# Four low halves of the output weights: subtracted on VectorE in round 0, where GpSimd subtracted them in the first routing

## The chip, the cores and the metric

The kernel runs on one core of a Trainium2 chip, as one program. The metric is device time in microseconds (us), from launch to end; the profile's span runs from the first to the last instruction and is a little shorter. The engines are TensorE (PE; PEld is its weight load), VectorE (DVE), ScalarE (ACT), GpSimd (POOL) and SyncE (SP, which issues plain DMAs). Each engine works through its own queue in order.

## The reference, cut to what matters

Three stages follow each other. The tokens are 3072 rows of 320 numbers.

```python
# 1. recurrent attention, 4 x 8 heads, 768 steps, head size 40  -> x[3072, 320]
# 2. routing: each token to one of 8 experts, at most 384 tokens each
logits = x @ w_gate
order = np.argsort(-logits.flatten())
for idx in order:
    tok, e = idx // 8, idx % 8
    if assigned[tok] >= 0 or counts[e] >= 384: continue
    assigned[tok] = e; counts[e] += 1
for e in range(8):
    out[assigned == e] = np.maximum(x[assigned == e] @ w1[e], 0) @ w2[e]   # 320 -> 1024 -> 320
# 3. a dense layer for all tokens
h = out @ w_in                                          # 320 -> 2048
g = np.where(h > 0, h, np.exp(np.minimum(h, 0)) - 1)
y = g @ w_out                                           # 2048 -> 320
```

`w_in` and `w_out` arrive as 64-bit floats.

## The kernel before, in words

**Stages.** First the attention runs (24 units, to about 160 us). Then the first routing finds the expert that is filled first and its 384 tokens. Then come eight rounds, one for each expert in the order in which they are filled. A round gathers its 384 rows of x and its expert's weights, does the expert's two matmul layers (P1 up, C1 down), and goes on at once with the dense layer for the same rows (P2 up, C2 down) and scatters the result. Routing r+1 is computed on VectorE beside round r.

**High and low halves.** For accuracy every matmul operand is split into a high part, which TensorE's reduced format holds exactly, and the low rest: h = round(F), l = F - h, with three products hh, lh and hl summed. So every weight and activation costs a copy (h) and a subtraction (l).

**The output weights.** `w_out` is cut into 16 pieces of 128x320. Since the chip gets 64-bit words, a piece is first rebuilt as 32-bit floats: ACT takes the exponent and the sign from the upper word (L867, L869), DVE shifts the lower word (L872) and joins the parts with an exclusive-or (L879), and GpSimd multiplies by the sign (L882), or DVE works the sign in with one more instruction (L876). Then ACT or DVE copies the high half (L980 or L982) and GpSimd subtracts the low half (L973). Pieces 0 to 6 (EARLY = 7) are done during the attention. Pieces 7 to 15 are done by the generator `wout_pieces`: as many as fit in the first routing, the rest in round 0. Round 0 needs piece f first in its C2 step f.

**The first routing.** It is a loop of counting steps: DVE compares all tokens with 32 thresholds (ge, L563, 128x768 bf16), TensorE counts, DVE folds the counts over the partitions (L587 to L593) and picks the next digit (L746, L749). `start` issues these steps, and wherever a step marks a gap for TensorE (k > FK) it advances `wout_pieces` up to its next stop for DVE; a yield's second value names the engines that the next part wants:

```python
while True:
    d = "d" in need
    _, need = next(fill)
    if d and "d" in need:
        break
```

When the routing has its expert, GpSimd gathers that expert's w1 (L991), then the rows of x.

**Order in the rounds.** A planner (`Plan`) keeps a clock and a booked time per engine (a, d, p), from fixed costs of each instruction, and the order of issue follows it. After `start` it is reset. `main` issues matmuls, two or a few per step; after each step `run` first issues the dependent work that is due (such as gl of P1, L1127) and then offers a turn to four side generators in the order `wout routes rows weights`. A generator's turn goes on as long as its next yield is not in the future and the engine that it names is not booked more than its slack ahead of the clock (wout 2000, weights 1000, routes and rows 3000 and 600). Between C1's last step and C2's first (`rush`) only routing may go on. `main` holds C2 of round 0 back until `wdone` says that the piece is issued. `weights` splits the gathered expert weights (L980, L987), `rows` gathers, transposes and splits the tokens of the next round (xh, xl, L1064).

Of the kernel before, what the change touches and what calls it, by code (L numbers as in the profile page):

```python
# [8 lines left out]
F32 = mybir.dt.float32  # L9
# [4 lines left out]
ALU = mybir.AluOpType  # L14
# [13 lines left out]
EARLY = 7  # L28
# [790 lines left out]
class Mlp:  # L819
# [128 lines left out]
    def wout_pieces(self):  # L948

        nc = self.nc  # L950
        wide = self.wout.dtype != F32
        n = 320
        tiles = {}

        def get(i):
            x = self.pool.tile([128, n, 2], I32, name="wx", bufs=3) if wide else None
            t = self.pool.tile([128, 2, n], F32, name="wt", bufs=2)
            tiles[i] = (x, t[:, 1], t[:, 0])
            self.fetch([(slice(0, 128), self.src(self.wout, slice(0, 128), slice(i * n, i * n + n)))], wide, tiles[i])

        get(EARLY)
        get(EARLY + 1)
        yield
        for i in range(EARLY, 16):
            if i < 14:
                get(i + 2)
            F = tiles[i][2]
            yield self.plan.t, "d"
            yield from self.conv(wide, tiles.pop(i), not self.router.res or self.plan.pick(p=890 + PD, d=484) == "p")
            h, l = self.wo(i)  # L970
            t = self.copy(h, F, 469, 310)
            yield t, "p"
            nc.gpsimd.tensor_tensor(l, F, h, op=ALU.subtract)  # L973
            self.plan.on("p", 880)
            self.wdone = i + 1

    def copy(self, out, x, a, d):

# [545 lines left out]
```

## Time and profile before

| what | value |
|---|---|
| three timed runs | 775.37, 776.09, 777.76 us (median 776.09) |
| the profiled execution | 770.57 us, span 768.6 us |
| TensorE busy | 708.4 us (92%), mean granted clock 0.961 |
| VectorE busy | 544.7 us (71%) |
| ScalarE busy | 381.8 us (50%) |
| GpSimd busy | 215.4 us (28%) |

Busy shares are means over all stages. The page's row of TensorE in 40 slices shows three parts: a busy attention (to 160 us), a hole of one or two slices (the first routing and the start of round 0, to about 196 us), and a full stretch up to the end. What ends an engine's idle time stands in square brackets or after an arrow in the views.

### The profile page before, as it was taken

To read this page: it belongs to the slowest core of one execution; us is meant where nothing else is said; L and a number is where in the kernel's file an instruction comes from. 1 tells how busy PE (TensorE), PEld (TensorE's weight loads), DVE (VectorE), ACT (ScalarE), POOL (GpSimd) and SP (SyncE) were. 2 spreads that over 40 slices of the span, in tenths; PEclk is the share of its full clock that TensorE was granted. 3 is DMA by queue.
4 is the path that set the end of the run, shared out by engine and by line. 5 is a ranking of instruction groups with operands and counts; after the bars stand their busy time and mean duration, and the time that the engine had idled before them with its cause. 6 is when DMAs were issued, how large, how long until landed. Compare 5 with 4: busy or idle time off the path is not lost.

```text
span 768.6 us, 18284 instructions
## 1 busy us (share of the span) xinstructions
PE 708.4 (92%) x7379; PEld 653.0 (85%) x7379; DVE 544.7 (71%) x1599; ACT 381.8 (50%) x817; POOL 215.4 (28%) x262
## 2 busy tenths in 40 slices
PE   7888887953999999999999999999999999999994
PEld 4766666742989998998999999999999999999994
DVE  8587777768878877886796589669768834841551
ACT  5645544423455635661673376257427734742542
POOL 4678766625211410401121030112023220001001
PEclk9989889975999999999999999999999999999998
DMA  7778968434300500500230041022013411100000
GB/s 279 240 252 258 294 212 267 117 91 159 118 1 1 182 27 1 179 5 27 81 102 27 1 126 57 26 84 100 1 36 110 141 61 35 35 1 27 0 1 26
DMA packets 23780, 72.79 MB, mean 95 GB/s; under 512 B 3536, under 2 KB 7632, under 8 KB 23696
## 3 DMA queue, kind: packets, MB, share of 16 engines
q1 hardware_dynamic: 15200, 39.80, 16.4%
q0 software_dynamic: 8448, 31.73, 12.4%
q8 instruction: 58, 0.95, 0.5%
q14 instruction: 26, 0.21, 0.1%
q10 hardware_dynamic: 48, 0.10, 0.0%
HBM read 62.96 MB, written 8.65 MB: 93 GB/s over the span
## 4 chain that ended last, share of the span: by engine, by line
PE 64%; issue 16%; DVE 11%; POOL 3%; ACT 3%; DMA 2%; SPq 0%; POOLq 0%; DVEq 0%; ACTq 0%
PE ph L1103 26%; PE acc L1242 5%; PE acc L1246 5%; PE acc L1243 5%; PE acc L1210 3%; PE acc L1212 2%; PE acc L1211 2%; PE pO L353 2%; PE pX L433 2%; PE pO L367 1%; PE acc L1197 1%; PE acc L1199 1%; DVE e L1156 1%; PE pC L379 1%; PE pX L423 1%
## 5 line engine op out<-in xcount | busy, mean ns | idle before, releaser
L1156 DVE SCALAR_TENSOR_TENSOR e<-e,ph 128x384 f32<-128x384 f32 x128 | 70.3, 550 | 55.6 <-ACT e L1153 52.4
L1152 ACT ACTIVATE e<-ph 128x384 f32<-128x384 f32 x128 | 62.5, 488 | 86.5 <-PE ph L1103 73.9
L1103 PE MATMUL ph<-yh,wih 128*128 128x384 f32 x256 | 89.8, 351 | 0.3
L1120 ACT ACTIVATE gh<-ph 128x384 fp32r<-128x384 f32 x64 | 31.4, 491 | 112.7 <-PE ph L1103 90.7
L1103 PE MATMUL ph<-yh,wil 128*128 128x384 f32 x256 | 86.7, 338 | 0.0
L1252 POOL DMA_INDIRECT out_dram<-ot,idx x24 | 24.1, 1004 | 210.1 <-ACT ot L980 207.1
L987 DVE TENSOR_TENSOR gl<-e,gh 128x384 fp32r<-128x384 f32 x128 | 70.9, 561 | 1.7 <-issue 0.3
L1153 ACT ACTIVATE e<-e 128x384 f32<-128x384 f32 x128 | 67.3, 526 | 4.0
L1242 PE MATMUL acc<-woh,gh 128*128 128x320 f32 x216 | 68.1, 315 | 0.0
L1127 DVE SCALAR_TENSOR_TENSOR gl<-ph,gh 128x384 fp32r<-128x384 f32 x64 | 35.2, 553 | 46.1 <-ACT gh L1120 45.6
L1243 PE MATMUL acc<-wol,gh 128*128 128x320 f32 x216 | 66.7, 309 | 0.0
L1246 PE MATMUL acc<-woh,gl 128*128 128x320 f32 x216 | 66.7, 309 | 0.0
L1103 PE MATMUL ph<-yl,wih 128*128 128x384 f32 x256 | 66.6, 341 | 0.0
L991 POOL DMA_INDIRECT stg<-in_w1a_dram,wi x16 | 15.7, 983 | 148.4 <-DVE wi L760 135.0
L980 ACT ACTIVATE gh<-e 128x384 fp32r<-128x384 f32 x97 | 49.4, 515 | 11.2 <-DVE e L1156 10.9
L1246 PE MATMUL acc<-woa,gl 128*128 128x320 f32 x168 | 52.4, 312 | 0.8 <-DVE gl L987 0.8
L1242 PE MATMUL acc<-woa,gh 128*128 128x320 f32 x168 | 53.1, 316 | 0.0
L1243 PE MATMUL acc<-wob,gh 128*128 128x320 f32 x168 | 51.9, 309 | 0.0
L1103 PEld LDWEIGHTS ph<-yh,wih 128*128 128x128 f32 x256 | 48.2, 188 | 4.1 <-ACT yh L1215 4.1
L1103 PEld LDWEIGHTS ph<-yh,wil 128*128 128x128 f32 x256 | 48.2, 188 | 0.0
L1103 PEld LDWEIGHTS ph<-yl,wih 128*128 128x128 f32 x256 | 46.2, 188 | 0.0
L1103 PE MATMUL ph<-xh,w1h 128*128 128x384 f32 x128 | 45.0, 352 | 0.0
(268 smaller groups left out, 2097.8 us busy)
## 6 DMA issues: line engine op xcount, KB each, us to landing
qk<-in_qk_dram SPq DMA_DIRECT2D x24, 512.0 KB, 5.7
vk<-in_vk_dram SPq DMA_DIRECT2D x24, 484.0 KB, 4.5
xd<-x SPq DMA_DIRECT2D x48, 96.0 KB, 3.0
cx<-in_win_dram SPq DMA_DIRECT2D x8, 512.0 KB, 6.2
wx<-in_wout_dram SPq DMA_DIRECT2D x9, 320.0 KB, 3.2
cx<-in_wout_dram SPq DMA_DIRECT2D x5, 448.0 KB, 6.4
cx<-in_win_dram SPq DMA_DIRECT2D x4, 256.0 KB, 6.3
xg<-xd,idx POOLq DMA_INDIRECT x24
```

The source lines that it names most:

```text
L980: self.nc.scalar.activation(out, x, AF.Copy)
L987: self.nc.vector.tensor_tensor(out, x, y, op=ALU.subtract)
L1103: PE.matmul(p, w, x, start=k == 0, stop=k == 7)
L1120: nc.scalar.activation(h, p, AF.Relu)
L1127: nc.vector.scalar_tensor_tensor(l, p, 0.0, h, op0=ALU.max, op1=ALU.subtract)
L1152: nc.scalar.activation(e, p, AF.Relu, scale=-1.0)
L1153: nc.scalar.activation(e, e, AF.Exp, scale=-1.0)
L1156: nc.vector.scalar_tensor_tensor(e, e, -1.0, p, op0=ALU.add, op1=ALU.max)
L1242: PE.matmul(p, h[:, c], wh, start=f == 0, stop=False)
L1243: PE.matmul(p, h[:, c], wl, start=False, stop=False)
L1246: PE.matmul(p, l[:, c], wh, start=False, stop=f == 15)
L1252: s = nc.gpsimd.indirect_dma_start(out=self.out, out_offset=bass.IndirectOffsetOnAxis(ap=idx[:, t:t + 1], axis=0), in_=o, in_offset=None)
```

## The change

The generator keeps each piece's rebuilt values for longer and has two ways on from the copy of the high half. In a routing before any result is there (`self.router.res` is empty) the low half is not subtracted; the piece is put on a list. Once the first routing is over (`routed >= 0`) the list is emptied behind the next piece, with one subtraction on DVE for each, booked at 390. Pieces 7, 8 and 9 keep their values in the three buffers of the output tile `ot`; a further one keeps them where it had them, in `wt`. `wdone` is set by each subtraction as it is issued.

```diff
             t = self.pool.tile([128, 2, n], F32, name="wt", bufs=2)
-            tiles[i] = (x, t[:, 1], t[:, 0])
+            keep = self.pool.tile([128, n], F32, name="ot", bufs=3) if i < EARLY + 3 else t[:, 0]
+            tiles[i] = (x, t[:, 1], keep)
...
+        late = []
...
             t = self.copy(h, F, 469, 310)
-            yield t, "p"
-            nc.gpsimd.tensor_tensor(l, F, h, op=ALU.subtract)
-            self.plan.on("p", 880)
-            self.wdone = i + 1
+            if self.router.res:
+                yield t, "p"
+                nc.gpsimd.tensor_tensor(l, F, h, op=ALU.subtract)
+                self.plan.on("p", 880)
+                self.wdone = i + 1
+            else:
+                yield t, ""
+                late.append((l, F, h, i))
+            while late and self.routed >= 0:
+                l, F, h, k = late.pop(0)
+                yield self.plan.t, "d"
+                self.minus(l, F, h, 390)
+                self.wdone = k + 1
```

`minus` issues `nc.vector.tensor_tensor(out, x, y, op=ALU.subtract)` and books its cost for DVE.

## Rows read from the trace of the kernel before

**Rows 1.** Windows by stage: length, busy us (instructions) by engine, granted PE clock, DMA.
```profile
160.00:196.30 36.30, 13.79 (x108) 10.15 (x109) 28.84 (x116) 12.68 (x27) 15.73 (x17) 0.58 0.47 146
196.30:222.00 25.70, 25.70 (x156) 24.45 (x156) 21.73 (x68) 10.90 (x24) 5.36 (x6) 0.99 0.17 54
222.00:246.00 24.00, 23.53 (x169) 21.93 (x168) 20.95 (x71) 15.41 (x32) 2.71 (x3) 1.00 0.01 2
246.00:270.00 24.00, 23.30 (x162) 22.37 (x161) 21.16 (x73) 15.11 (x31) 9.71 (x12) 1.00 0.43 147
270.00:340.00 70.00, 69.66 (x470) 66.07 (x469) 57.98 (x191) 38.64 (x81) 9.50 (x12) 1.00 0.18 58
```

**Rows 2.** Chain of waits, first routing: start us, us, what.
```profile
169.09 0.56 DVE ge L563
...
171.93 1.11 DVE ge L563
...
175.32 1.10 DVE ge L563
...
178.70 1.10 DVE ge L563
...
188.31 0.24 DVE inc L814
188.55 3.60 DMA xg<-xd,idx
```

**Rows 3.** Timeline of GpSimd in the first routing: start, us, instruction, idle before.
```profile
170.28 0.87 POOL L882 TENSOR_TENSOR wt<-wt,wx 128x320 f32<-128x320 f32 x1 [9.49 <-DVE wt L879]
171.72 0.90 POOL L973 TENSOR_TENSOR wol<-wt,woh 128x320 fp32r<-128x320 f32 x1 [0.58 <-ACT woh L980]
...
175.11 0.90 POOL L973 TENSOR_TENSOR wol<-wt,woh 128x320 fp32r<-128x320 f32 x1 [0.58 <-ACT woh L980]
...
178.50 0.89 POOL L973 TENSOR_TENSOR wol<-wt,woh 128x320 fp32r<-128x320 f32 x1 [0.58 <-ACT woh L980]
...
181.86 0.86 POOL L973 TENSOR_TENSOR wol<-wt,woh 128x320 fp32r<-128x320 f32 x1 [0.58 <-ACT woh L980]
183.63 1.14 POOL L991 DMA_INDIRECT stg<-in_w1a_dram,wi  x1 [0.90 <-DVE wi L760]
```

**Rows 4.** Timeline of DVE: the same instruction in the first and second routing.
```profile
182.12 0.64 DVE L768 SCALAR_TENSOR_TENSOR AB<-d,j,a 128x24 f32<-128x24 f32 x1
...
247.60 0.23 DVE L768 SCALAR_TENSOR_TENSOR AB<-d,j,a 128x24 f32<-128x24 f32 x1
```

**Rows 5.** DVE's groups by line and shape: busy us, mean ns, idle before.
```profile
L987 DVE TENSOR_TENSOR gl<-e,gh 128x384 fp32r<-128x384 f32 x128 | 70.9, 561 | 1.7 <-issue 0.3
...
L987 DVE TENSOR_TENSOR w<-stg,w 128x256 fp32r<-128x256 f32 x16 | 6.6, 413 | 0.0
...
L879 DVE SCALAR_TENSOR_TENSOR wt<-wt 128x320 int32<-128x320 int32 x9 | 4.3, 483 | 0.2
...
L872 DVE TENSOR_SCALAR wt<-wx 128x320 int32<-128x320 int32 x9 | 2.8, 311 | 0.0
```

**Rows 6.** Timeline of DVE at the start of round 0.
```profile
200.66 0.55 DVE L1127 SCALAR_TENSOR_TENSOR gl<-ph,gh 128x384 fp32r<-128x384 f32 x1
201.13 0.32 DVE L872 TENSOR_SCALAR wt<-wx 128x320 int32<-128x320 int32 x1
201.36 0.42 DVE L987 TENSOR_TENSOR w<-stg,w 128x256 fp32r<-128x256 f32 x1
```

**Rows 7.** Timeline of TensorE: first down-projection of round 0; start of round 1.
```profile
202.11 0.33 PE L1195 MATMUL acc<-gh,w 128*128 128x384 f32 x1
...
269.50 0.61 PE L1103 MATMUL ph<-xl,w1h 128*128 128x384 f32 x2 [0.70 <-DVE xl L1064]
```

**Rows 8.** Windows around the start of round 0, columns as in Rows 1.
```profile
194.00:196.00 2.00, 2.00 (x7) 1.26 (x6) 0.89 (x2) 0.98 (x2) 0.68 (x1) 0.50 0.90 256
...
196.50:197.00 0.50, 0.50 (x4) 0.50 (x4) 0.50 (x3) 0.00 (x0) 0.00 (x0) 0.86 1.03 225
```

## The prediction, made before the changed kernel was run

> **What bounds the kernel now.** I first read the windows by stage [rows 1]. From 196.3 us on TensorE is busy all the time: 25.70 of 25.70 us in the first stretch of round 0, 23.53 and 23.30 of 24 in the next two, 69.66 of 70 in the next stretch, and the five 70 us stretches after it look the same. Whatever happens there is paid only as a TensorE wait. Before it, in the stretch of the last attention unit and the first routing (160 to 196.3 us), TensorE has 13.79 us of work in 36.3 and VectorE 28.84: that stretch is a serial chain, and the reader should see that DVE, not PE, carries it.
>
> The chain of waits says the same [rows 2]: one DVE instruction after the other to 188.55 us, then the gather of the token rows (DMA, 3.60 us), then transposes and the first matmul of round 0. In the chain the comparison ge (L563) is 0.56 us at 169.09 and 1.11, 1.10 and 1.10 us the next three times. GpSimd's timeline [rows 3] shows what stands beside the slow ones: the four subtractions of L973, at 171.72, 175.11, 178.50 and 181.86, each 0.86 to 0.90 us. The slow ge's start 0.2 us after one of the first three and end at 173.04, 176.42 and 179.80; those subtractions end at 172.62, 176.01 and 179.39. Every slow ge thus ends 0.41 or 0.42 us after "its" subtraction, as if most of it had only begun when GpSimd was done. The fourth subtraction (to 182.72) meets AB (L768) [rows 4]: 0.64 us at 182.12, against 0.23 for the same instruction in the next routing.
>
> By the Trainium skill ("SBUF — State Buffer", its parts on the shared GpSimd/Vector port) a DVE instruction with two SBUF inputs and a GpSimd one that reads SBUF hold one port pair by turns, whole instructions at a time, the later one blocked until the other ends; the ends 0.41 us behind agree with that, but the rule cuts both ways, since the four new DVE subtractions have two SBUF inputs as well.
>
> **What the change removes.** Four pieces, 7 to 10, get to their subtraction in the first routing (four rows ahead of the gathers) [rows 3]. Gone from the chain are 1.11 - 0.56 = 0.55, twice 1.10 - 0.56 = 0.54, and 0.64 - 0.23 = 0.41 us: **2.04 us**. The multiplication of L882 (0.87 us at 170.28, one per piece) stays; it follows its DVE input and lies beside the short fold instructions, so that the next ge still starts when GpSimd is free. What is late next is again DVE: nothing else ends near these ge's. The gathers of w1 (from 183.63) wait for wi, a DVE result, with GpSimd idle before them [rows 3]; they and the row gather move up by the same time, and so does round 0. Their own durations I leave as they are. No DMA is added or moved: get(i+2) stays where it is, SP's queue is untouched, and GpSimd's gathers only have fewer instructions ahead. Three kept halves lie in buffers of the output tiles, which are not used before the end of round 0; I cost that at nothing, and were it not free a wait of ACT or DVE on a buffer would show in the routing.
>
> **What it adds.** Four DVE subtractions of 128x320. The trace has no such one; the same operation takes 0.413 us for 256 and 0.561 for 384 elements a partition [rows 5]. Between them, 0.48 us. Instructions in a row overlap: the one at 200.66 is 0.55 long and the next starts after 0.47 [rows 6], so each costs the queue 0.40 us, **1.6 us** in all. It is paid only where TensorE ends up waiting.
>
> Where they go is the planner's business. They are drained right behind piece 11, which is resumed in the first up-projections. Before, piece 12's shift (L872) is issued there, right behind the first gl (L1127) [rows 6]; its place is now that of the first late ones. The planner stops the generator when its booking for DVE is over 2,000 ahead of its clock; by its own costs (used for the order alone) the booking there is just under 1,600 ahead, so one brings it to 1,990, a second to 2,380, and the third and fourth wait for a shorter booking. So two stand ahead of the last split of the first w2 piece (L987, 201.36 to 201.78), in place of a shift that held the queue for 0.23 us: 2 x 0.40 - 0.23 = 0.57 us later, so 202.35 on the old clock. The first down-projection matmul (L1195, 202.11) reads that split [rows 7]. That is a wait of 0.24, with a semaphore **0.3 us**. Ends: 0, if other DVE work moves behind, and 4 x 0.40 - 0.23 = 1.37 us later, a wait of 1.04, if all four go in one burst. I take 0.3, because the booking rule stops it at two.
>
> Queued behind them on DVE are the other gl's of round 0 (they have the length of a down-projection's lag to spare), the splits of w2, and the second routing. Pieces 12 to 15 are pushed back by about one piece, which moves a shift and an exclusive-or (0.31 and 0.48 us) [rows 5, 6] into the later, fuller part of round 0, where DVE is busy 20.95 and 21.16 of 24 us [rows 1]. The weak spot is the start of round 1: there TensorE already waits 0.70 us for xl, a DVE result [rows 7]. A queue longer by one piece's shift and exclusive-or makes that 0.31 + 0.48 = 0.79 later if nothing absorbs it; half of it, **0.4 us**, is my value, since DVE still has some 6 us free in those 48 us. Ends: -0.70 (another order lets the wait vanish) and +1.6 (all the added DVE time comes out there). From 270 us on I cost the change at nothing: there TensorE hides all, with 0.34 us of idle time in 70 [rows 1], and if that cover is gone a late split shows as a wait.
>
> **Sum.** -2.04 + 0.3 + 0.4 = -1.34 us. The profiled execution is 770.57 us (span 768.60 and 1.97 around it), which gives 769.2; the timed runs of before lie 5.5 us above it at the median, with 2.4 us between the lowest and the highest, and I take the difference over to the median: 776.09 - 1.34 = 774.75, say **774.8**. From the bounds: -2.04 - 0.70 = -2.74 to -2.04 + 1.04 + 1.6 = +0.6.
>
> **Rivals.**
> 1. *All of it comes through.* The waits of 0.3 and 0.4 don't appear because the reordered queue has air, or the 0.70 us at round 1 goes too: -2.0 to -2.7 us, 773.4 to 774.1. For it: 9.9 us of idle DVE time between 196.3 and 270 (73.7 us less 63.84 busy) [rows 1]. Against: the idle time is elsewhere than at these two places, where DVE runs without a gap.
> 2. *The clock does not move with the work.* The granted clock is 0.50 from 194 to 196 us, while the transposes run, and reaches full speed in 196.5 to 197 (mean 0.86 there) [rows 8], when round 0's matmuls have just begun. Should it rise at the same time as before while the matmuls start 2.04 us sooner, that much work runs at 1.2 instead of 2.4 GHz: it does half and 1.02 us are lost. Then -1.34 + 1.02 = -0.32, 775.8. For it: nothing in the trace ties the rise to the first matmul. Against: the work ahead of it moves up as a block, and the rise may follow it. The Trainium skill ("TensorE: Matmul & The Clock Gate", "What's actually happening") says the activity window runs free and so the moment varies from run to run; one trace cannot show that. By it either side can win by about a microsecond, in both kernels alike.
> 3. *The queue pays it all back (slower).* The four go in one burst ahead of the w2 split (1.04 us) and the same 1.6 us of DVE time comes out again in front of xl at the start of round 1: -2.04 + 1.04 + 1.6 = +0.6, 776.7. If the second routing is also held back by one step of the main loop, up to five matmuls of 384 columns (0.16 us each at 2.4 GHz), another 0.8 us: +1.4, 777.5. It decides once the waits added in round 0 exceed 2.04 us. For it: DVE is the engine with the least air in round 0, and a late routing delays everything of round 1. Against: the stop at 2,000 and only 1.6 us of added work. A DVE subtraction that meets GpSimd's work on pieces 11 to 15 would be held up to 0.9 us (as ge was held 0.55), the same sign.
> 4. *It does not do what it says.* ge is slow for another reason that coincides with L973; then 0 + 0.7, 776.8. Against: the first two ge's, with no subtraction beside them, are both fast.
>
> **How the numbers follow.** Forecast 0.58, rival 1 0.18, rival 2 0.12, rival 3 0.10, rival 4 0.02. A change of 0.3% (2.33 us), about what a measurement of this kernel can tell from none, is more than the 2.04 us that the routing can give; "faster" by that much needs rival 1 with the vanished wait, or scatter on top of the forecast: 0.17. "Slower" by it needs rival 3 and more than its priced form: 0.06. The rest, 0.77, is within 0.3%. Range: rival 1's far end, 773.4, to rival 3's far end less the part left out, 776.8, each with some tenths for the scatter of the runs: 773.1 to 777.0.
>
> **What would show it.** All ge's of the first routing at about 0.56 us and AB at 0.23; no GpSimd instruction but four multiplications in it; the first up-projection matmul at 194.3 instead of 196.3 us; four DVE subtractions into wol, two of them between the first gl and the last split of the first w2 piece; a TensorE wait of some tenths at L1195, and one near 1.1 us at the start of round 1. It is wrong if ge stays at 1.1 us, if the transposes don't move up with idx, or if TensorE shows over 2 us of new waits between the start of round 0 and that of round 1.

## The result, and the profile after

The changed kernel takes **781.13 us** (median of 12 runs, 777.27 to 784.29); the kernel before, run beside it, 776.12 (12 runs, 773.09 to 780.36). The ratio is 1.006 with a 95% interval of 1.0039 to 1.0081: 0.6% slower, where 774.8 had been forecast with a range of 773.1 to 777.0. The prediction was wrong.

The profiled execution took 783.17 us, with a span of 781.3. It can't be set against the 768.6 of before as it stands, because the attention, whose instructions the change doesn't touch, takes a different time in every run. Here are the first 160 us of three executions, the kernel before, the kernel before once more, and the changed one, columns as in [rows 1]:

```profile
0.00:160.00 160.00, 134.02 (x3603) 105.87 (x3603) 119.87 (x268) 82.11 (x192) 109.22 (x133) 0.93 0.74 233
```

```profile
0.00:160.00 160.00, 133.66 (x3401) 105.98 (x3401) 110.73 (x244) 81.15 (x184) 104.21 (x129) 0.85 0.72 230
```

```profile
0.00:160.00 160.00, 134.24 (x3496) 107.33 (x3502) 117.61 (x255) 80.81 (x187) 106.71 (x131) 0.85 0.73 230
```

The same program had a granted clock of 0.93 once and 0.85 once, and its first routing began at 164.85 and at 175.61 us. So I compare traces from one instruction on, the first digit of the first routing (DVE fl L735; at 171.25 us in the changed kernel). From there to the end the two profiles of before take 603.75 and 604.29 us, the two of after 610.05 and 609.02: 5.5 us more at the mean. The timed medians differ by 5.0. They carry the attention's scatter; the figures taken from this instruction on ("anchored" below) don't.

**Where it was won.** The chain of waits of the changed kernel in the first routing, then DVE's timeline at its end (columns as in [rows 2, 4]):

```profile
175.49 0.56 DVE ge L563
...
178.33 0.56 DVE ge L563
...
181.16 0.56 DVE ge L563
...
183.99 0.56 DVE ge L563
...
192.40 0.24 DVE inc L814
192.63 5.38 DMA xg<-xd,idx
```

```profile
186.88 0.23 DVE L768 SCALAR_TENSOR_TENSOR AB<-d,j,a 128x24 f32<-128x24 f32 x1
...
187.46 0.22 DVE L760 SCALAR_TENSOR_TENSOR wi<-mul,m,add 128x3 int32<-128x3 f32 x1
...
188.66 0.18 DVE L790 TENSOR_SCALAR hl<-iv 128x24 int32<-128x24 int32 x1
```

Every ge is at 0.56 and AB at 0.23, where [rows 2, 4] have 1.11, 1.10, 1.10 and 0.64. From fl to inc the routing takes 21.15 us, before 23.46. The row gather behind inc, though, takes 5.38 us in this profile, where [rows 2] have 3.60.

**Where it was lost.** GpSimd's timeline at the first gather, DVE's at the start of round 0 and in the second routing, and the last window of [rows 1], all of the changed kernel:

```profile
185.17 0.86 POOL L882 TENSOR_TENSOR wt<-wt,wx 128x320 f32<-128x320 f32 x1 [1.95 <-ACT wx L869]
188.62 1.14 POOL L1002 DMA_INDIRECT stg<-in_w1a_dram,wi  x1 [2.59 <-DVE inc L785]
```

```profile
206.66 0.55 DVE L1138 SCALAR_TENSOR_TENSOR gl<-ph,gh 128x384 fp32r<-128x384 f32 x1
207.12 0.88 DVE L998 TENSOR_TENSOR wol<-ot,woh 128x320 fp32r<-128x320 f32 x2
207.93 0.42 DVE L998 TENSOR_TENSOR w<-stg,w 128x256 fp32r<-128x256 f32 x1
...
214.81 0.48 DVE L998 TENSOR_TENSOR wol<-ot,woh 128x320 fp32r<-128x320 f32 x1
215.21 0.48 DVE L998 TENSOR_TENSOR wol<-wt,woh 128x320 fp32r<-128x320 f32 x1
...
258.79 0.21 DVE L760 SCALAR_TENSOR_TENSOR wi<-mul,m,add 128x3 int32<-128x3 f32 x1
```

```profile
270.00:340.00 70.00, 65.04 (x427) 60.88 (x426) 55.13 (x185) 33.92 (x72) 13.43 (x18) 0.98 0.25 82
```

The first gather of w1 starts 1.16 us behind its input wi (187.46 to 188.62), before 0.51 (183.12 to 183.63). The second routing's wi comes at 258.79, which is 56.56 us behind the first up-projection matmul of round 0 (202.23); before it was 52.15 behind, as these two lines of the kernel before show (TensorE, then DVE):

```profile
196.13 0.61 PE L1103 MATMUL ph<-xh,w1h 128*128 128x384 f32 x1
```

```profile
248.28 0.22 DVE L760 SCALAR_TENSOR_TENSOR wi<-mul,m,add 128x3 int32<-128x3 f32 x1
```

And from 270 to 340 us TensorE, which had been busy for 69.66 of 70 us [rows 1], is busy for 65.04, at a clock of 0.98. The holes are at the start of round 1. TensorE's timeline in the changed kernel (the first up-projection matmul of round 0, the first of round 1 and its first down-projection):

```profile
202.23 0.45 PE L1114 MATMUL ph<-xh,w1h 128*128 128x384 f32 x1
...
275.34 0.45 PE L1114 MATMUL ph<-xh,w1h 128*128 128x384 f32 x1 [0.64 <-ACT xh L991]
...
277.39 0.62 PE L1114 MATMUL ph<-xl,w1h 128*128 128x384 f32 x2 [1.08 <-DVE xl L1075]
...
284.92 0.18 PE L743 MATMUL pr<-flag,onz 128*128 128x8 bf16 x1 [2.14 <-DVE flag L593]
285.85 0.44 PE L1206 MATMUL acc<-gh,w 128*128 128x384 f32 x1 [0.76 <-DVE w L998]
```

The idle 2.14 us is put down to flag, a product of the third routing that ended last; what TensorE's next matmul of the round needs is w, the split of w2. The chain of waits there runs through w2's data (start, us, what):

```profile
277.83 4.23 DMA stg<-in_w2a_dram,wi
282.08 0.64 ACT w L991
...
285.85 0.44 PE acc L1206
```

And w2's gathers are late because of what stands ahead of them on GpSimd. Its timeline before:

```profile
260.93 0.94 POOL L991 DMA_INDIRECT stg<-in_w2a_dram,wi  x1 [0.31 <-ACT w1h L980]
264.19 1.02 POOL L991 DMA_INDIRECT stg<-in_w2a_dram,wi  x1 [2.32 <-DVE w1l L987]
...
267.98 1.42 POOL L1252 DMA_INDIRECT out_dram<-ot,idx  x1 [2.68 <-ACT ot L980]
```

After:

```profile
269.38 0.94 POOL L1002 DMA_INDIRECT xg<-xd,idx  x1 [0.30 <-issue]
...
273.92 1.00 POOL L1263 DMA_INDIRECT out_dram<-ot,idx  x1 [3.51 <-ACT ot L991]
...
276.55 0.97 POOL L1263 DMA_INDIRECT out_dram<-ot,idx  x1 [0.22 <-issue]
...
277.83 0.98 POOL L1002 DMA_INDIRECT stg<-in_w2a_dram,wi  x1 [0.30 <-issue]
279.11 1.16 POOL L1002 DMA_INDIRECT stg<-in_w2a_dram,wi  x1 [0.30 <-issue]
```

Before, both gathers go ahead of round 0's scatter of the results. After, they are issued behind all three scatters, whose first waits 3.51 us for the output tile ot, with GpSimd idle and w2's gather queued behind it. The windows of the changed kernel around the hole show the rest of the price, in the clock:

```profile
282.00:284.00 2.00, 0.78 (x5) 0.46 (x3) 1.22 (x3) 1.92 (x5) 0.00 (x0) 1.00 0.76 277
284.00:286.00 2.00, 0.33 (x2) 0.25 (x3) 1.87 (x8) 1.79 (x5) 0.00 (x0) 1.00 0.00 0
286.00:288.00 2.00, 2.00 (x10) 1.96 (x11) 1.93 (x6) 0.34 (x2) 0.00 (x0) 0.79 0.00 0
288.00:290.00 2.00, 2.00 (x8) 2.00 (x7) 1.31 (x4) 0.00 (x0) 0.00 (x0) 0.50 0.00 0
290.00:292.00 2.00, 2.00 (x16) 1.84 (x16) 0.56 (x1) 0.59 (x2) 0.00 (x0) 0.86 0.00 0
```

TensorE works for 0.78 and 0.33 of 2 us, still at full clock; when it works again, the clock falls to 0.50, which is 1.2 GHz, and comes back about 4 us later. Over the 20 us behind the first down-projection of round 1 the mean clock is 0.91 in both profiles of the changed kernel and 1.00 in both of before. That is 1.8 us of work at full speed, and "rest" in the table below is 1.5 us longer.

The sum by stages is in the table. All differences are taken within one trace, from the start of one instruction to that of another. "Routing" is fl to inc (L814), "to P1" from there to the first up-projection matmul of round 0, "round 0" from there to the first one of round 1, "to C1" from there to the first down-projection of round 1, "rest" from there to the end. "wi" is from the first up-projection matmul of round 0 to the wi of the second routing (a part of "round 0").

| profile | routing | to P1 | round 0 | to C1 | rest | fl to end | wi |
|---|---|---|---|---|---|---|---|
| before | 23.46 | 7.82 | 71.81 | 6.82 | 493.84 | 603.75 | 52.15 |
| before2 | 23.45 | 8.04 | 71.98 | 6.87 | 493.95 | 604.29 | 52.33 |
| after | 21.15 | 9.83 | 73.11 | 10.51 | 495.45 | 610.05 | 56.56 |
| after2 | 21.13 | 8.94 | 73.11 | 10.44 | 495.40 | 609.02 | 56.57 |
| e3_booking_only | 23.44 | 8.64 | 73.10 | 10.63 | 496.73 | 612.54 | 56.56 |
| e1_unbooked | 21.13 | 9.18 | 73.10 | 6.83 | 493.96 | 604.20 | 53.46 |
| e2_w2_early | 21.13 | 9.07 | 72.98 | 7.67 | 494.03 | 604.88 | 56.42 |
| e4_later | 21.13 | 9.32 | 71.91 | 6.85 | 493.96 | 603.17 | 52.25 |
| e5_ot_only | 23.19 | 8.79 | 71.63 | 6.82 | 493.92 | 604.35 | 51.98 |
| e6_early_wait | 21.41 | 8.28 | 72.03 | 6.83 | 493.86 | 602.41 | 52.37 |
| e7_book300 | 21.13 | 9.02 | 73.87 | 7.07 | 493.83 | 604.92 | 55.76 |
| e8_book300_wait | 21.40 | 7.41 | 74.55 | 6.88 | 493.89 | 604.13 | 56.22 |

After less before, means of two profiles each: -2.31 + 1.46 + 1.21 + 3.63 + 1.53 = **+5.5 us**.

### The profile page after: what moved, and what is told of

It reads as the page before. It is cut to its first block, busy times and chain, and to the rows that moved or that the text cites. A ratio compares the mean times of both kernels' runs of the same rounds, so it can differ in the third digit from the quotient of the medians.

```text
span 781.3 us, 18279 instructions
## 1 busy us (share of the span) xinstructions
PE 717.6 (92%) x7375; PEld 661.6 (85%) x7379; DVE 546.0 (70%) x1605; ACT 381.1 (49%) x815; POOL 211.2 (27%) x257
## 4 chain that ended last, share of the span: by engine, by line
PE 64%; issue 18%; DVE 9%; POOL 3%; ACT 3%; DMA 1%; POOLq 0%; DVEq 0%; ACTq 0%
PE ph L1114 25%; PE acc L1253 5%; PE acc L1257 5%; PE acc L1254 5%; PE acc L1221 2%; PE pO L353 2%; PE acc L1223 2%; PE acc L1222 2%; PE pX L433 2%; PE pO L367 2%; PE pC L379 1%; PE acc L1208 1%; PE pX L423 1%; PE acc L1210 1%; DVE w L998 1%
```

## The experiments

Three theories stood against each other. The *bookings*: the 4 x 390 ns that the planner now books for DVE hold back the second routing, whatever DVE really does. The *work*: the four subtractions themselves delay DVE. The *buffers*: the new tiles in `ot`, which I had costed at nothing, move something. Four kernels were run first, on one chip, beside the kernel before (775.52 us, 25 runs).

**The subtractions without the booking.** The change, but the late list is emptied at once, with no stop in between and nothing told to the planner:

```diff
                 l, F, h, k = late.pop(0)
-                yield self.plan.t, "d"
-                self.minus(l, F, h, 390)
-                self.wdone = k + 1
+                nc.vector.tensor_tensor(l, F, h, op=ALU.subtract)
```

> The changed kernel, but the four DVE subtractions go out in one burst behind piece 11 without being booked in the planner, so that every other instruction keeps the order of the kernel before (round 1's w2 gathers stay ahead of the scatters of round 0). Spans are compared from the first count of the first routing (the DVE instruction fl, L735) to the end: 603.75 us before, 610.05 after. Theory A (the planner's order is the loss: the booking makes the second routing late, the w2 gathers fall behind the scatters and TensorE waits at the first down-projection of round 1): no wait there; about 603 to 605 us (-2.3 routing, +1.6 slower gather, about +1 at the first down-projection of round 0); timed within 0.3% of the kernel before. Theory B (the 1.6 us of DVE time is the loss: the queue is full and it comes out in front of round 1): still 608 to 611 us, timed 0.4 to 0.8% slower than the kernel before.

The time was 777.92 us (12 runs), ratio 1.004 (1.0014 to 1.0065). In the trace the second routing's wi comes 53.46 us after the first up-projection instead of 56.56, and round 1's down-projection follows 6.83 us after the up-projection, as before. DVE's timeline, then TensorE's, where the round 0 down-projection starts:

```profile
204.11 1.28 DVE L984 TENSOR_TENSOR wol<-ot,woh 128x320 fp32r<-128x320 f32 x3
205.32 0.48 DVE L984 TENSOR_TENSOR wol<-wt,woh 128x320 fp32r<-128x320 f32 x1
...
205.95 0.41 DVE L996 TENSOR_TENSOR w<-stg,w 128x256 fp32r<-128x256 f32 x1
```

```profile
206.42 0.44 PE L1204 MATMUL acc<-gh,w 128*128 128x384 f32 x1 [1.25 <-DVE w L996]
```

All four go in one burst, and TensorE waits 1.25 us for the split behind them: that is the prediction's burst (1.04), and it accounts for round 0's 73.10. So the same DVE work, unbooked, costs round 1 nothing: the wait for xl at its start is 0.70 us again, as in [rows 7]. Anchored, this kernel is within 0.5 us of before, which the timed 0.4% does not bear out; what makes up that difference is open.

**The booking without the subtractions.** The kernel before, with GpSimd subtracting in the first routing as ever, but with the stops and bookings of the change:

```diff
-            yield t, "p"
+            early = not self.router.res
+            yield t, "" if early else "p"
             nc.gpsimd.tensor_tensor(l, F, h, op=ALU.subtract)
...
+            if early:
+                late.append(i)
+            else:
+                self.wdone = i + 1
+            while late and self.routed >= 0:
+                k = late.pop(0)
+                yield self.plan.t, "d"
+                self.plan.on("d", 390)
+                self.wdone = k + 1
```

> The kernel before, GpSimd subtracting in the first routing, with only the planner's bookings and yields of the change added: 4 x 390 for DVE behind piece 11, and no instruction for them. Theory A (order): the w2 gathers of round 1 stand behind the scatters as in the changed kernel, TensorE waits 3 to 5 us at the first down-projection of round 1, span from fl to the end 607 to 609 us, timed 0.4 to 0.8% slower. Theory B (DVE time): nothing is added to DVE, span 603 to 604.5 us, timed the same.

782.15 us (6 runs), ratio 1.0085 (1.006 to 1.0109). None of the four subtractions is on DVE (it has 1601 instructions against 1599, because the planner moved two others to it, as it does in the changed kernel), the routing keeps its 23.44 us, and yet wi comes at 56.56 us and the down-projection of round 1 at 10.63, as in the changed kernel. GpSimd's timeline has the same order, and the windows the same clock:

```profile
274.66 0.97 POOL L1262 DMA_INDIRECT out_dram<-ot,idx  x1 [0.22 <-issue]
275.93 0.98 POOL L1001 DMA_INDIRECT stg<-in_w2a_dram,wi  x1 [0.30 <-issue]
```

```profile
286.00:288.00 2.00, 2.00 (x8) 2.00 (x7) 1.53 (x4) 0.00 (x0) 0.00 (x0) 0.50 0.00 0
```

Anchored it takes 612.54 us, more than the 607 to 609 expected, in part because the clock stays at half speed for longer ("rest" 496.73). That settles the work against the bookings: the loss comes without the work and goes without the booking. It clears the buffers of it too, since this kernel has none of the new ones.

**w2 fetched earlier.** The change, with the two w2 gathers of round 1 issued behind the first two w1 splits, not behind the third:

```diff
                 yield from self.split_w(i)
+                if r == 1 and i < 2:
+                    self.get_w(r, 3 + i)
                 if i == 2:
-                    self.get_w(r, 3)
-                    self.get_w(r, 4)
+                    if r > 1:
+                        self.get_w(r, 3)
+                        self.get_w(r, 4)
```

> The changed kernel with its bookings, but in round 1 alone the two w2 gathers are issued right after the first and the second w1 split, ahead of round 0's scatters. Theory A: the wait of TensorE at round 1's first down-projection (0.76 us at the matmul and 3 to 4 us behind it in the waits for w2's DMA) is gone, span from fl to the end 605 to 607 us. Theory B: unchanged within 1 us, 609 to 611 us.

778.73 us (8 runs), ratio 1.0041 (1.0009 to 1.0073), which the timing alone can't tell from the change's 1.006; anchored it takes 604.88, where after has 610.05 and 609.02. The gathers are ahead of the scatters again, although wi is as late as ever (56.42):

```profile
271.08 0.94 POOL L1002 DMA_INDIRECT stg<-in_w2a_dram,wi  x1 [0.30 <-issue]
274.06 1.27 POOL L1002 DMA_INDIRECT stg<-in_w2a_dram,wi  x1 [2.04 <-DVE w1l L998]
275.64 1.09 POOL L1263 DMA_INDIRECT out_dram<-ot,idx  x1 [0.22 <-ACT xh L991]
```

"To C1" is 7.67 and "rest" 494.03: 2.8 of the 3.6 us of waiting and all of the clock's 1.5 are gone. The late routing does most of its harm through these two gathers' place in GpSimd's queue. "Round 0" stays at 72.98.

**The subtractions later, unbooked.** As the first of these kernels, but spread: the one in `wt` at once, the three in `ot` only behind piece 12:

```diff
-            while late and self.routed >= 0:
-                l, F, h, k = late.pop(0)
+            while late and self.routed >= 0 and (late[-1][3] == EARLY + 3 or i > EARLY + 4):
+                l, F, h, k = late.pop(-1 if late[-1][3] == EARLY + 3 else 0)
```

> As the unbooked version, but only piece 10's subtraction goes behind piece 11; those of 7, 8 and 9 go behind piece 12, where DVE was idle for 1.4 us before (at 214.6 us). Theory A: about 0.5 to 1 us less than the unbooked version, since no burst stands ahead of the last split of the first w2 piece: 602 to 604 us from fl to the end, timed 0 to 0.4% faster than the kernel before. Theory B: as slow as the changed kernel, 608 to 611 us, since the same DVE time is added.

774.32 us (12 runs), ratio 0.998 (0.9954 to 1.0005); anchored 603.17. The three go in a row at 210.64 us, for 1.28 us (0.43 each), behind the first down-projection, and TensorE does not wait for them: "round 0" is 71.91, as before. What is left against the routing's gain is "to P1", 9.32 (from inc to round 0's first up-projection).

**The buffers alone.** The kernel before with the one line that puts the kept values of pieces 7 to 9 into `ot`, one run, beside second profiles of before and after:

```diff
-            tiles[i] = (x, t[:, 1], t[:, 0])
+            keep = self.pool.tile([128, n], F32, name="ot", bufs=3) if i < EARLY + 3 else t[:, 0]
+            tiles[i] = (x, t[:, 1], keep)
```

> The kernel before, GpSimd subtracting in the first routing, with only the values of pieces 7 to 9 moved to the output tiles' buffers. If the other place of the buffers causes the later gather: from wi to the first gather 1.16 us instead of 0.51, transposes 0.6 us or more later, from fl to the end 604.0 to 605.0 us. If the missing GpSimd subtraction causes it: 0.51 us and 603.3 to 604.2.

> The kernel before once more, for how much two profiles of one program differ: routing from fl to inc 23.4 to 23.5 us, from fl to the end 603.2 to 604.8; the attention ahead of fl differs by several us, as its program is the same in all these kernels.

> The changed kernel once more: routing 21.1 to 21.2 us, from fl to the end 609.0 to 610.8 us, w2 gathers of round 1 behind the scatters, first down-projection of round 1 10 to 11 us behind its first up-projection.

The times of the single runs were 779.94, 781.8 (before) and 782.31 us (after); they say little, the traces more. DVE's wi and GpSimd's first gather in the kernel with the buffers alone:

```profile
191.91 0.22 DVE L760 SCALAR_TENSOR_TENSOR wi<-mul,m,add 128x3 int32<-128x3 f32 x1
```

```profile
193.07 1.15 POOL L992 DMA_INDIRECT stg<-in_w1a_dram,wi  x1 [1.55 <-DVE iv L786]
```

The gather starts 1.16 us after wi: the changed kernel's delay, from the buffers alone. The wait instructions in the traces, which the views leave out, show how. Before, the gather itself carries the wait for DVE's event. Here it carries a wait for an event of TensorE, and the one for DVE's stands in an instruction of its own, with a second wait instruction 0.68 us behind it and the gather 0.22 us behind that. My reading, which no trace shows, is that tiles allocated earlier shift all later ones, so that the first `stg` buffer lands where an attention tile was. The buffers also give something: hl (L790) takes 0.18 us here, where it starts 0.04 us into the later gather, and 0.43 us before, where it starts 0.69 us into it. The routing takes 23.19 us with all four GpSimd subtractions in it. The two profiles of before agree within 0.6 us from fl on, those of after within 1.0, and nearly all of that 1.0 is "to P1". What the delay is worth shows over all twelve traces: the first transpose of the gathered rows starts 3.76 to 4.10 us behind inc in the five whose gather starts 0.51 us behind wi, and 4.76 to 5.65 in the seven where it is 1.16, which is 1.1 us at the mean.

**The wait taken earlier.** The spread kernel, with the first `stg` tile allocated at the start of the first routing and one column of it written by GpSimd, so that the TensorE event is waited for there:

```diff
+        self.stg0 = [self.pool.tile([128, 1280], F32, name="stg", bufs=3)]
+        nc.gpsimd.memset(self.stg0[0][:, 1279:], 0.0)
...
-        s = self.pool.tile([128, 1280], F32, name="stg", bufs=3)[:, :n]
+        s = (self.stg0.pop() if self.stg0 else self.pool.tile([128, 1280], F32, name="stg", bufs=3))[:, :n]
```

> The version with the subtractions of 7, 8 and 9 behind piece 12, in which GpSimd also writes one word of the first gather's buffer at the start of the first routing, so that the wait for that memory (a TensorE event of the attention, long past) is done early and the first w1 gather waits for wi in its own instruction, as before the change. Theory C (a second wait ahead of the gather, in an instruction of its own, costs 0.65 us): from wi to the first gather 0.5 us again instead of 1.16; the first transposes 4.0 to 4.4 us after the routing's last result instead of 4.9 to 5.7; from fl to the end 602.2 to 602.8 us, timed 0.1 to 0.5% faster than the kernel before. Rival D (the gathers' DMA sets the start of round 0, whatever the issue): gather issued sooner, but the transposes stay 4.9 us or more behind the routing; 603 to 603.5 us.

The gather is at 0.51 us behind wi (181.32) again, and carries the wait for DVE's event itself:

```profile
181.83 1.15 POOL L1000 DMA_INDIRECT stg<-in_w1a_dram,wi  x1 [1.93 <-DVE wi L760]
```

"To P1" falls from 9.32 to 8.28, the routing rises by 0.28 (hl is at 0.43 us once more), and the anchored time is 602.41, the lowest of all: 1.3 and 1.9 us under the two profiles of before. Timed, it is 775.51 against 776.48 (12 and 17 runs), ratio 0.9999 (0.9976 to 1.0023): not to be told from no change.

**A smaller booking.** The change with 300 booked for each subtraction instead of 390, and the same with the early wait:

```diff
-                self.minus(l, F, h, 390)
+                self.minus(l, F, h, 300)
```

> The changed kernel with one number altered: each late subtraction is booked at 300 instead of 390. The same four DVE subtractions, buffers and yields; in the order of issue that comes out, the w2 gathers of round 1 stand ahead of round 0's scatters again. Theory A (the order is the loss, and it tips at a size of the booking): the first down-projection of round 1 comes 6.8 us behind the first up-projection instead of 10.5, no drop of the granted clock behind it; from fl to the end 603.5 to 605.5 us, timed 0.5 to 0.8% below the changed kernel, within 0.4% of the kernel before. Theory B (DVE's added time is the loss): 609 to 610 us as the changed kernel.

> As the booking of 300, with GpSimd's early word in the first gather's buffer as well (the first gather waits for wi in its own instruction). If the two repairs add up: another 0.65 to 1.0 us less, from fl to the end 602.5 to 604.8 us, timed the same as the kernel before within 0.3%. If the gather's issue did not matter, as the booking of 300 within 0.3 us.

776.19 us (12 runs) against 776.85, ratio 1.0001 (0.997 to 1.0032), and 777.09 with the early wait, ratio 1.0009 (0.998 to 1.0038); anchored 604.92 and 604.13. The first interval ends below where that of the change begins (1.0039): a constant in the planner, with the same four subtractions and stops, is worth the loss. w2's gathers are ahead of the scatters (268.17 and 271.08 us, the first scatter at 274.13), "to C1" is 7.07 and "rest" 493.83. Where between 300 and 390 the order tips was not run. wi is still late (55.76), and "round 0" is even longer (73.87, 74.55): with 300, TensorE waits 0.63 us at its first down-projection and 0.73 us for a flag of the routing.

## Why the prediction was wrong, point by point

- **The routing's gain (-2.04)** was right: 23.46 - 21.41 = 2.05 us where the first gather is not delayed (e6_early_wait). The changed kernel gains 0.26 to 0.28 more, mostly at hl, which was not in the sum. By the Trainium skill ("SBUF — State Buffer", "Who interferes with whom") a DVE instruction with two SBUF inputs contends with a GpSimd one that reads SBUF, over a port pair that they share; ge's fall from 1.10 to 0.56 with GpSimd's subtraction gone agrees. The new DVE subtractions took 0.48 us each, the estimate, and none was held.
- **The buffers "at nothing"** was wrong. I had looked for a wait on the `ot` buffers themselves; the cost came at the first gather, 0.65 us later (1.16 - 0.51, shown by e5_ot_only), and grew to 1.1 us at the transposes. "To P1" is 1.46 us longer in all; the rest is within what varies from run to run (0.9 us between the two profiles of after).
- **+0.3 at the first down-projection of round 0:** right in kind. Two subtractions stand ahead of the split, as the stop at 2,000 said, and the distance from up- to down-projection grew by 0.15 us (6.03 to 6.18, means of two). Four in a burst cost 1.25 (e1_unbooked), near the upper bound.
- **+0.4 at the start of round 1:** right for xl by luck. The wait for xl grew from 0.70 [rows 7] to 1.08 us, but not because DVE's queue was longer by one piece: with the work and no booking it is 0.70 (e1_unbooked), with the booking and no subtraction 1.08 (e3_booking_only). It is the late routing, which adds a wait of 0.64 us for xh that the sum did not have. "Round 0" grew by 1.21 us: 0.64 of it is that wait, 0.15 the item above, and the rest is not attributed.
- **"From 270 us on I cost the change at nothing" is the step that failed.** It costs 3.63 + 1.53 = 5.2 us, 0.38 of them in the wait for xl above. The step named the risk (a late split shows as a wait) but took the cover for given. I reckoned how far DVE's queue gets longer by the added instructions; I did not ask what the added *bookings* do to the generators that share DVE's clock. The second routing fell behind, wi came 4.3 us later (56.57 less 52.24, means of two), and two gathers, the second of which had been 3.8 us ahead of the first scatter (264.19 to 267.98), were issued behind all three. Then TensorE stood idle for 2.14 and 0.76 us and lost its clock.
- **Rival 3** had the place, the second routing held back by a step of the loop, at 0.8 us; the delay was 4.3, and it came out in the waits for xh and xl and above all as a changed order. The range ended at its priced form (whose sum, +0.6, gives 776.7 and not the 776.8 in the text).
- **Rival 2** didn't decide: the clock's cost came in round 1, behind a hole, not at round 0's start. Over the first 3 us of round 0 the granted clock was 0.91 and 1.00 in the two profiles of before, a difference worth some 0.3 us, and 1.00 in both of after.
- **Where the second routing falls behind** can be read from the traces. Its comparisons (ge) start 28.4, 34.8, 40.9, 46.9 and 51.4 us behind the first up-projection of round 0, where before they start at 28.0, 34.3, 39.4, 43.5 and 47.4. So it loses its time from about 35 us on, and not where the four subtractions are issued (5 and 13 us). It loses it beside the last three pieces, whose GpSimd subtractions lie at 36.7, 42.5 and 47.1 us, before at 18.3, 32.5 and 37.8. They went back by one place, as forecast, with two that are now abreast of the routing's last steps; e3_booking_only has the same times. That these pieces take the routing's turns is argued, not shown.
- **Left open:** why 1.56 us of bookings grow to 4.3 us of delay there; why two kernels (e1_unbooked and e2_w2_early) time 0.4% slower with an anchored time 0.2 and 0.9 us above before; and whether the 1.3 to 1.9 us of e6_early_wait are there, since the attention's scatter is larger.

## What to carry to other kernels

Where a planner orders the issue, a booked cost is itself a change: ask which other generators share that engine's clock, and look for the place where two queue entries stand close to swapping, above all a gather and a scatter that waits. When a sum of small terms comes out at a microsecond or two, the tail is set by such swaps, so the range on the slow side should hold one of them at the price of the wait and of the clock behind it. And compare traces from an instruction behind the part that scatters: here that part alone differed by 10.8 us between two executions of one program, twice the change's whole effect.

## What the runs showed of the hardware that was not expected

- **A hole is paid twice.** In the changed kernel TensorE was idle for 2.14 and 0.76 us, with little between; the granted clock was still 1.00 then and fell to 0.50 when work had resumed (286 to 290 us), worth another 1.5 us in both profiles of after and 2.8 in e3_booking_only, where it was down to 0.85 already in the hole (282 to 284 us). A single idle time of 1.25 us (e1_unbooked) was followed by a clock of 1.00. The Trainium skill ("TensorE: Matmul & The Clock Gate", "What's actually happening") has the clock set by how busy the array has been, which agrees.
- **Where a wait stands matters.** The first gather starts 1.16 us behind wi in the seven traces where the wait for wi is in an instruction of its own, ahead of it, and 0.51 us in the five where the gather carries that wait itself.
- **A small integer instruction can be slow beside a gather:** hl (128x24) takes 0.43 us in the five traces where it starts 0.69 us into GpSimd's first indirect gather, and 0.18 in the seven where it starts 0.04 us into it. The line of before:

```profile
184.32 0.43 DVE L790 TENSOR_SCALAR hl<-iv 128x24 int32<-128x24 int32 x1
```

- **One program, two speeds:** in two executions of the kernel before, the first 160 us had a mean granted clock of 0.93 and 0.85, and the first routing began 10.8 us apart.
